# Attention and a two-layer network in one kernel: dummy matmuls, two attention blocks and two copies rearranged

## The chip, the cores and the metric

The kernel runs on one core of a Trainium2 chip. A core has TensorE (matmuls, written PE, with its weight loads as PEld), VectorE (DVE), ScalarE (ACT), GpSimd (POOL) and SyncE (SP), which run side by side and wait for each other by semaphores, and 16 DMA engines fed from queues on SP and POOL. Matmul results go to PSUM, which has eight banks of 2 KB for each of 128 partitions; everything else is in SBUF. The metric is the device time of one execution in microseconds; lower is better.

## The reference

What is computed, for 8 batches, 8 heads, 576 positions and 64 values per head:

```python
q_s = softmax(q, over the 64 values of a head)        # per position
k_s = softmax(k, over the 576 positions)              # per value
kv  = einsum('bhsd,bhse->bhde', k_s, v)               # 64 x 64 per head
x   = einsum('bhsd,bhde->bhse', q_s, kv)              # as 4608 rows of 512
h   = x @ w_in                                        # 512 x 2048
out = maximum(0.01 * h, h) @ w_out                    # 2048 x 512
```

Inputs and output are 4-byte floats. The softmaxes subtract their maximum first.

## The kernel before, in words

The 4608 rows are cut into nine blocks of 512 (NT; index t). The two matrices of the network stay in SBUF in bf16, and so does xT, the attention's output transposed. For a block, layer 1 makes 16 tiles of h (j = 0 to 15, each four matmuls, `layer1`), ScalarE applies the leaky function from PSUM to SBUF (`leaky`, tile gj), and layer 2 sums 16 matmuls for each of four groups of 128 rows (`layer2`, tsub 0 to 3) into a bank called pout; the result is copied by VectorE or ScalarE (`store`) and sent out from SP's queue.

A batch has 576 rows, so blocks and batches don't line up: block t has the last rows of batch t-1 and the first rows of batch t. The first stage takes all 576 rows of batch 0 (16 tiles of 256 columns in two halves, then 16 of 320); its last 64 rows are carried over to block 1 by `g_carry`, eight small POOL copies.

The attention of a batch: maxima and subtraction for k and q (VectorE and POOL), exponentials (ScalarE), v cast to bf16 with a column of ones (`v_cast`, tile vb), key-value product and sums of k on TensorE (`kv`, 36 small matmuls into two banks), their quotient (`kd_make`, tile kd, VectorE), q normalised and transposed by a DMA from SP's queue (`q_turn`, tile qX), and eight matmuls for the output (`attend_x`, two row ranges XR of 5 and 4 of the nine row groups, four head pairs each; tile po), each of which ScalarE or VectorE casts into xT. Batch 0 does its transposes on TensorE (`q_transpose`, `q_keep`) and its outputs in `attend`.

The order of all this is written out by hand. No scheduler moves anything: each engine runs its instructions in the order of the program. `at(t, u, ...)` hangs functions on a place in the loops, and `run(t, u)` calls them there. For t = 0, u is 0 to 15 in the 256-column stage, 16 to 31 in the 320-column stage and 32 to 47 in layer 2 (one u for each j, which is four matmuls). For later blocks u is 0 to 15 in layer 1 and 16 to 31 in layer 2 (four matmuls each). `plan2` hangs batch 2's steps on block 1, `plan` those of batches 3 to 7 on later blocks.

PSUM is in two pools: psB with six banks (name tag "bank2k": h tiles, po, key-value products, transposes) and psO with two (pout). In block 0 layer 2 sums four row groups at once: two in psO and two in psB (pout2), which leaves four psB banks for anything else until those are copied out.

Before the first real matmuls TensorE has dummies: `wake(n)` issues n bf16 matmuls of zeros, 128x512, into a bank that nobody reads, and `wake_on(x, n)` does the same behind a small matmul that reads x, so that it starts when x is there.

Of the kernel before, what the change touches and what calls it, by code (L numbers as in the profile page):

```python
# [8 lines left out]
FP32 = mybir.dt.float32  # L9
# [16 lines left out]
def kernel(  # L26
# [9 lines left out]
    nc = tc.nc  # L36
# [10 lines left out]
    P = 128  # L47
    NB = C // P
    NF = F // P
    TT = 512  # L50
# [4 lines left out]
    const_pool = ctx.enter_context(tc.tile_pool(name="const", bufs=1))  # L55
# [12 lines left out]
    psO_pool = ctx.enter_context(tc.tile_pool(name="psO", bufs=2, space=bass.MemoryType.PSUM))  # L68
# [19 lines left out]
    st = [{} for _ in range(B)]  # L88
# [15 lines left out]
    identf = const_pool.tile([P, P], FP32)  # L104
# [2 lines left out]
    nc.gpsimd.memset(block, 0.0)  # L107
    for p0 in range(0, P, D):
        nc.gpsimd.memset(block[p0 : p0 + D, p0 : p0 + D], 1.0)
    warm = const_pool.tile([P, 1], BF16)  # L110
    nc.scalar.activation(out=warm, in_=ident[:, 0:1], func=AF.Exp)
    gate = const_pool.tile([P, 1], FP32)
# [117 lines left out]
    def q_first(b, rs):  # L230

        n = rs.stop - rs.start
        nmax = small_pool.tile([P, HL, n], FP32, name="nmax")
        qsum = small_pool.tile([P, n, HL], FP32, name="qsum")
        for hs in (slice(0, 2), slice(2, 4)):
            nc.vector.tensor_reduce(
                out=nmax[:, hs], in_=st[b]["q"][:, hs, rs], axis=AX.X, op=ALU.max, negate=True
            )
            for h in range(hs.start, hs.stop):
                for r in range(n):  # L240
                    nc.scalar.activation(
                        out=st[b]["qe"][:, rs.start + r, h],
                        in_=st[b]["q"][:, h, rs.start + r],
                        func=AF.Exp,
                        bias=nmax[:, h, r : r + 1],
                        accum_out=qsum[:, r, h : h + 1],
                    )
        st[b]["qsum"] = qsum
        st[b]["nmax"] = nmax
# [41 lines left out]
    def kv(b):  # L291

        pkv = [psB_pool.tile([P, 2, 130], FP32, name="pkv", tag=BANK_TAG) for _ in range(2)]
        for gg in range(2):
            for r in range(R):
                for hh in range(2):
                    rows = slice(hh * L, (hh + 1) * L)
                    nc.tensor.matmul(  # L298
                        pkv[hh][:, gg, 0:129],
                        lhsT=st[b]["ke"][rows, r, 2 * gg : 2 * gg + 2].rearrange(  # L300
                            "p h d -> p (h d)"
                        ),
                        rhs=vb2[b % 2][rows, r, gg, 0:129],
                        start=(r == 0),
                        stop=(r == R - 1),
                    )
        st[b]["pkv"] = pkv

    def kd_make(b):
        for hh in range(2):  # L310
            pkv = st[b]["pkv"][hh]
            krec = small_pool.tile([P, 2, 1], FP32, name="krec")
            nc.vector.reciprocal(out=krec, in_=pkv[:, :, 128:129])
            for hp in range(2):
                p0 = hp * D
                nc.vector.tensor_tensor(
                    out=kd2[b % 2][p0 : p0 + D, 2 * hh : 2 * hh + 2, p0 : p0 + D],
                    in0=pkv[p0 : p0 + D, :, p0 : p0 + D],
                    in1=krec[p0 : p0 + D].to_broadcast([D, 2, D]),
                    op=ALU.mult,  # L320
                )

    wake_ps = psO_pool.tile([P, TT], FP32, name="pout")

    def wake(n):
        for i in range(n):
            nc.tensor.matmul(  # L327
                wake_ps, lhsT=zero[:, 0:P], rhs=zero, start=(i == 0), stop=(i == n - 1)
            )

    def wake_on(x, n):

        nc.tensor.matmul(wake_ps[:, 0:8], lhsT=identf, rhs=x, start=True, stop=True)
        wake(n)

    def k_max_pe(b, i):
        ps = psB_pool.tile([P, 2, L], FP32, name="kT", tag=BANK_TAG)
# [71 lines left out]
    def q_keep(eng, b, r0, n, ggs=(0, 1)):  # L409
        for gg in ggs:  # L410
            o, i = st[b]["qT", gg][:, :, r0 : r0 + n], st[b]["ps", r0][:, gg::2]
            if eng is nc.scalar:
                eng.copy(out=o, in_=i)
            else:
                eng.tensor_copy(out=o, in_=i)

    def attend(b, gs, c0, n, eng, pool=psB_pool, tag=BANK_TAG):

        ps = pool.tile([P, len(gs), n], FP32, name="po", tag=tag)
        for i, g in enumerate(gs):  # L420
            nc.tensor.matmul(
                ps[:, i],
                lhsT=kd2[b % 2][:, g],
                rhs=st[b]["qT", g % 2][:, g // 2].rearrange("c r l -> c (r l)")[:, c0 : c0 + n],
                start=True,
                stop=True,
            )
        x0 = XB[gs[0]]
        o = xT[:, x0 : x0 + len(gs), b * S + c0 : b * S + c0 + n]
        if eng is nc.scalar:  # L430
            eng.copy(out=o, in_=ps)
        else:
            eng.tensor_copy(out=o, in_=ps)
# [10 lines left out]
    def attend_x(b, g, rs, eng):  # L444
        hh, gg = divmod(g, 2)
        n = (rs.stop - rs.start) * L
        ps = psB_pool.tile([P, n], FP32, name="po", tag=BANK_TAG)
        qX = st[b]["qX"].rearrange("c (r g) (h l) -> c g h r l", g=2, h=2)
        nc.tensor.matmul(  # L449
            ps.rearrange("p (r l) -> p r l", l=L), lhsT=kd2[b % 2][:, g], rhs=qX[:, gg, hh, rs]  # L450
        )
        c0 = b * S + rs.start * L
        o = xT[:, XB[g], c0 : c0 + n]
        if eng is nc.scalar:
            eng.copy(out=o, in_=ps)  # L455
        else:
            eng.tensor_copy(out=o, in_=ps)
# [11 lines left out]
    def leaky(o, ph):  # L469
        nc.scalar.activation(out=o, in_=ph, func=AF.Prelu, alpha=LEAKY_SLOPE)  # L470
# [22 lines left out]
    def at(t, u, *fns):  # L493
        while t > 0 and u >= 32:
            t, u = t + 1, u - 32
        hooks.setdefault((t, u), []).extend(fns)
# [14 lines left out]
    XR = (slice(0, 5), slice(5, R))  # L511
# [3 lines left out]


    HA, HB = slice(0, 1), slice(1, 2)
    wake(13)
    nc.gpsimd.tensor_copy(out=gate[:, 0:1], in_=st[0]["k"][:, HL - 1, R - 1, D - 1 : D])
    load_w_in(0, 8)  # L520
    k_begin(0)
    q_begin(0)
    q_first(0, RA)
    wake_on(st[0]["nmax"].rearrange("p h r -> p (h r)")[:, 8:16], 3)
    k_tree(0, H0)
    k_max_pe(0, 0)
    wake(1)
# [10 lines left out]
    v_cast(nc.gpsimd, 0, 1)  # L538
    k_all_dve(0, 1)
    k_all_pe(0, 1)  # L540
    wake(5)
    k_sub_ps(0, 0, HB)
    k_exp(0, slice(1, 2))
    v_cast(nc.scalar, 0, 0)
# [36 lines left out]
        load_w_out(slice(j0, j1))  # L581


    at(0, 11, lambda: attend(0, [0, 2], 256, 256, nc.scalar))
    at(0, 11, lambda: attend(0, [1, 3], 256, 256, nc.vector))
    at(0, 11, lambda: attend(0, [0, 2, 1, 3], 512, 64, nc.scalar, psO_pool, "pout"))
    at(0, 15, lambda: k_begin(1), lambda: q_begin(1), lambda: k_tree(1, H0), lambda: k_tree(1, H1))
    at(0, 15, lambda: q_max(1, XR[0]), lambda: q_sub(nc.gpsimd, 1, XR[0]), lambda: k_allmax(1))
    at(0, 15, lambda: k_sub(nc.vector, 1, H0), lambda: k_sub(nc.vector, 1, H1))
# [5 lines left out]
    at(0, 39, lambda: kv(1), lambda: q_sum(1, XR[1]), lambda: q_norm(1, XR[1]), lambda: kd_make(1))  # L595
    at(0, 43, lambda: q_turn(1, XR[1]), lambda: load_all(2))
    for i in range(8):
        eng = nc.vector if i in (5, 7) else nc.scalar
        at(0, 47, lambda i=i, eng=eng: attend_x(1, i % 4, XR[i // 4], eng))


    for b in range(3, B):
# [20 lines left out]
    def plan2():  # L623
        b = 2
        at(1, 0, lambda: k_begin(b), lambda: q_begin(b), lambda: k_tree(b, ALLH))
        at(1, 3, lambda: k_allmax(b))
        at(1, 6, lambda: k_sub(nc.vector, b, H0), lambda: k_sub(nc.vector, b, H1))
        at(1, 12, lambda: k_exp(b, ALLH))
        for rs in XR:
            at(1, 9, lambda rs=rs: q_max(b, rs), lambda rs=rs: q_sub(nc.gpsimd, b, rs))  # L630
        at(1, 13, lambda: v_cast(nc.gpsimd, b, 0), lambda: v_cast(nc.gpsimd, b, 1))
        for i, rs in enumerate(XR):
            at(1, (15, 16)[i], lambda rs=rs: q_exp(b, rs), lambda rs=rs: q_sum(b, rs), lambda rs=rs: q_norm(b, rs))
            at(1, (16, 17)[i], lambda rs=rs: q_turn(b, rs))
        at(1, 21, lambda: kv(b))
        at(1, 22, lambda: kd_make(b))
        for i in range(8):
            at(1, 28 + i // 2, lambda i=i: attend_x(b, i % 4, XR[i // 4], nc.scalar))

# [13 lines left out]
            g_next.append(g_tile())  # L653
            nc.gpsimd.tensor_copy(out=g_next[jj][:, :, 0:L], in_=g_sb[jj][:, :, TT : TT + L])

    at(0, 46, g_carry)
    begun = []

    def begin(j):
# [12 lines left out]
    for j in range(0, NF, 2):  # L672
        if j == 8:
            q_transpose(0, 4, 2)
            for jj in range(8, NF, 2):
                begin(jj)
            q_keep(nc.vector, 0, 4, 2)
            q_transpose(0, 6, 3)
            q_keep(nc.vector, 0, 6, 3)
        ph = begun.pop(0)  # L680
        for i in range(2):
            layer1(j + i, ph[:, i], 0, 256, slice(2, 4), i == 0, i == 1)
            if i == 1:
                leaky(g_sb[j // 2][:, :, 0:256], ph)
            run(0, j + i)
# [5 lines left out]
    pout = [psO_pool.tile([P, O], FP32, name="pout") for _ in range(2)]  # L691
# [66 lines left out]
```

## Time and profile before

| what | value |
|---|---|
| median of three runs | 291.18 us (291.14 to 291.42) |
| profiled execution | 291.04 us |
| its span, first to last instruction | 289.2 us |
| granted TensorE clock, mean | 1.000 |
| TensorE busy | 279.7 us (97%) |
| ScalarE, VectorE, POOL busy | 148.2, 148.5, 85.6 us |
| HBM read, written | 36.70 MB, 9.44 MB |

The profile is of one execution. Times are microseconds from the first instruction. A line of a timeline has the start, the busy time, the engine, the line of the kernel, the operation, output and inputs, sizes, the count of instructions merged, and in brackets the idle time of the engine before it with what ended it. A record of a matmul goes from its start until its result has left the array, so neighbouring records overlap; the step from start to start is what a matmul takes in a stream (0.2155 us for 512 columns, 0.109 for 256). In a merged line the shape is that of the first instruction.

What waited for what on TensorE, added up over the run: the first dummy for POOL's zeros 1.3 us; the transpose of k's maxima for VectorE 0.9; batch 0's key-value product for ScalarE's cast of v 0.8; the broadcast of the maxima 0.7; layer 1 for w_in's load 0.7; batch 2's key-value product for POOL's cast of v 0.4; the dummies behind nmax 0.4; layer 1 for xT 0.2.

### The profile page before, as it was taken

The numbers are of one execution on the slowest core, as the hardware profiler recorded it, in microseconds if no ns is written. First come the engines' busy times: TensorE is split into PE (matmuls) and PEld (weight loads), VectorE is DVE, ScalarE is ACT, GpSimd is POOL, SyncE is SP. The second block draws the span as 40 slices with busy tenths as digits, with TensorE's granted clock in tenths as the row PEclk, the third lists the DMA queues.
The fourth block names the chain that finished last, engine by engine and source line by source line (L and its number), as shares of the span: only waits on it lengthen the run. The fifth ranks groups of instructions, "written<-read, shape, count | busy, mean of one in ns | idle before, by whom it ended". The sixth has DMA issues, their size and how long they took to land.

```text
span 289.2 us, 4274 instructions
## 1 busy us (share of the span) xinstructions
PE 279.7 (97%) x1646; PEld 138.5 (48%) x1646; DVE 148.5 (51%) x246; ACT 148.2 (51%) x273; POOL 85.6 (30%) x70
## 2 busy tenths in 40 slices
PE   7689999999999999999999999999999999999995
PEld 2277654454444544454454544444454444444443
DVE  3997883896880994388175637554631200110011
ACT  4976870785269307922774358433953066016400
POOL 4735460017059009505900590039100000000000
PEclk9999999999999999999999999999999999999999
DMA  7999996987749174953397239913141310131033
GB/s 257 314 208 378 258 189 186 399 293 296 148 108 399 62 154 118 398 133 76 78 381 187 50 82 348 239 36 73 39 82 36 75 36 1 36 82 29 0 72 75
DMA packets 38932, 46.35 MB, mean 160 GB/s; under 512 B 18304, under 2 KB 21632, under 8 KB 38912
## 3 DMA queue, kind: packets, MB, share of 16 engines
q1 hardware_dynamic: 35456, 41.75, 48.5%
q0 software_dynamic: 3296, 4.20, 8.3%
q8 instruction: 13, 0.21, 0.3%
q10 hardware_dynamic: 160, 0.13, 0.1%
q14 instruction: 7, 0.06, 0.1%
HBM read 36.70 MB, written 9.44 MB: 160 GB/s over the span
## 4 chain that ended last, share of the span: by engine, by line
PE 74%; POOL 1%; ACT 0%; DVE 0%; issue 0%
PE pout L482 37%; PE ph L461 34%; PE pkv L298 2%; PE po L449 2%; POOL vb L216 1%; ACT xT L455 0%; DVE out_sb L476 0%
## 5 line engine op out<-in xcount | busy, mean ns | idle before, releaser
L482 PE MATMUL pout<-w_out_sb,gj 128*128 128x512 bf16 (+2 forms) x592 | 130.0, 373 | 0.0
L461 PE MATMUL ph<-xT,w_in_sb 128*128 128x512 bf16 (+3 forms) x640 | 127.5, 358 | 1.2 <-DMA w_in_sb<-in_moe_w_in_dram 0.7
L470 ACT ACTIVATE gj<-ph 128x512 bf16<-128x512 f32 (+2 forms) x152 | 83.6, 581 | 57.8 <-PE ph L461 55.8
L461 PEld LDWEIGHTS <-w_in_sb 128*128 128x128 bf16 x640 | 62.1, 98 | 63.5 <-issue 2.4
L482 PEld LDWEIGHTS <-gj 128*128 128x128 bf16 x592 | 57.0, 98 | 62.5
L476 DVE COPY out_sb<-pout 128x512 f32<-128x512 f32 (+1 forms) x34 | 22.7, 675 | 85.4 <-PE pout L482 82.5
L196 POOL TENSOR_TENSOR k_raw<-k_raw,kall 128x2304 f32<-128x2304 f32 x5 | 25.3, 5066 | 76.8 <-DVE kall L188 50.4
L455 ACT CAST xT<-po 128x320 bf16<-128x320 f32 (+1 forms) x54 | 18.8, 405 | 48.4 <-PE po L449 48.4
L259 POOL TENSOR_TENSOR q_raw<-q_raw,qmax 128x2304 f32<-128x2304 f32 (+3 forms) x10 | 29.7, 2974 | 22.4 <-DVE qmax L228 22.4
L276 DVE TENSOR_REDUCE qsum<-qe 128x36 f32<-128x2304 bf16 (+4 forms) x11 | 19.8, 1798 | 32.2 <-ACT qe L267 32.2
L283 DVE TENSOR_TENSOR qe<-qe,qrec 128x2304 bf16<-128x2304 bf16 (+4 forms) x12 | 21.9, 1826 | 0.4
L204 ACT ACTIVATE ke<-k_raw 128x2304 bf16<-128x2304 f32 (+2 forms) x11 | 17.5, 1595 | 8.7 <-POOL k_raw L196 8.5
L228 DVE TENSOR_REDUCE qmax<-q_raw 128x36 f32<-128x2304 f32 (+4 forms) x11 | 19.6, 1788 | 0.0
L267 ACT ACTIVATE qe<-q_raw 128x2304 bf16<-128x2304 f32 (+4 forms) x11 | 16.8, 1526 | 1.5 <-POOL q_raw L259 1.3
L216 POOL CAST vb<-v_raw 128x1152 bf16<-128x1152 f32 x13 | 14.6, 1147 | 0.0
L449 PE MATMUL po<-qX,kd 128*128 128x320 bf16 (+1 forms) x56 | 11.6, 286 | 0.3
L163 DVE TENSOR_TENSOR t<-k_raw 128x1024 f32<-128x1024 f32 (+1 forms) x10 | 10.1, 1011 | 0.5 <-DMA k_raw<-in_k_dram 0.2
L327 PE MATMUL pout<-zero 128*128 128x512 bf16 x28 | 8.9, 443 | 1.3 <-POOL zero L101 1.3
L163 DVE TENSOR_TENSOR t<-t 128x256 f32<-128x256 f32 (+2 forms) x20 | 9.6, 478 | 0.7
L476 ACT COPY out_sb<-pout 128x512 f32<-128x512 f32 (+1 forms) x3 | 1.6, 543 | 15.6 <-PE pout L482 15.6
L298 PE MATMUL pkv<-vb,ke 64*128 64x129 bf16 x252 | 8.5, 216 | 0.4 <-POOL vb L216 0.4
L298 PEld LDWEIGHTS <-ke 64*128 64x128 bf16 x252 | 7.2, 93 | 3.5 <-ACT gj L470 1.7
(61 smaller groups left out, 100.3 us busy)
## 6 DMA issues: line engine op xcount, KB each, us to landing
out_dram<-out_sb SPq DMA_DIRECT2D x70, 128.0 KB, 2.4
q_raw<-in_q_dram SPq DMA_DIRECT2D x7, 1152.0 KB, 8.2
v_raw<-in_v_dram SPq DMA_DIRECT2D x7, 1152.0 KB, 11.5
k_raw<-in_k_dram SPq DMA_DIRECT2D x6, 1152.0 KB, 5.8
k_raw<-in_k_dram SPq DMA_DIRECT2D x4, 576.0 KB, 5.6
w_in_sb<-in_moe_w_in_dram POOLq DMA_DIRECT2D x8, 256.0 KB, 7.1
v_raw<-in_v_dram SPq DMA_DIRECT2D x2, 576.0 KB, 7.4
w_out_sb<-in_moe_w_out_dram POOLq DMA_DIRECT2D x4, 256.0 KB, 9.4
```

The costliest lines, as they stand in the source:

```text
L163: nc.vector.tensor_tensor(out=o, in0=i0, in1=i1, op=ALU.max)
L196: eng.tensor_tensor(out=ks, in0=ks, in1=st[b]["kall"][:, hs].unsqueeze(2).to_broadcast([P, n, R, D]), op=ALU.subtract,)
L228: nc.vector.tensor_reduce(out=m, in_=st[b]["q"][:, :, rs], axis=AX.X, op=ALU.max)
L259: eng.tensor_tensor(out=qs, in0=qs, in1=st[b]["qmax", rs.start].unsqueeze(3).to_broadcast([P, HL, n, D]), op=ALU.subtract,)
L276: nc.vector.reduce_sum(out=qsum, in_=st[b]["qe"][:, rs], axis=AX.X)
L283: nc.vector.tensor_tensor(out=qes, in0=qes, in1=st[b]["qrec", rs.start].unsqueeze(3).to_broadcast([P, n, HL, D]), op=ALU.mult,)
L298: nc.tensor.matmul(pkv[hh][:, gg, 0:129], lhsT=st[b]["ke"][rows, r, 2 * gg : 2 * gg + 2].rearrange("p h d -> p (h d)"), rhs=vb2[b % 2][row ...
L455: eng.copy(out=o, in_=ps)
L461: nc.tensor.matmul(ph, lhsT=w_in_sb[:, cb, j * P : (j + 1) * P], rhs=xT[:, XB[cb], c0 : c0 + n], start=(i == 0 and first), stop=(i == NB - ...
L470: nc.scalar.activation(out=o, in_=ph, func=AF.Prelu, alpha=LEAKY_SLOPE)
L476: copy(out=out_sb, in_=pout)
L482: nc.tensor.matmul(pout, lhsT=g_sb[j // 2][:, j % 2, tsub * P : (tsub + 1) * P], rhs=w_out_sb[:, j, os], start=(j == 0), stop=(j == NF - 1),)
```

## The change

Five edits:

- The dummies. `wake(13)` becomes `wake(6)` and one matmul of 4-byte zeros (`wake32`); `wake_on` becomes a single 4-byte matmul that reads x through a broadcast to 512 columns; `wake(5)` becomes one `wake32`. POOL fills the 4-byte zeros (zerof) once at the start.
- Batch 0's late rows: ScalarE copies the first half of each transposed q (head pairs 0 and 2), VectorE the second; before, VectorE copied both. The attention of rows 256 to 575 of batch 0 is hung on u = 9 in place of 11, ahead of three more h tiles.
- Batch 1's attention: four matmuls after j = 13 of layer 2 (u = 45) and four after j = 14 (u = 46); before, all eight after j = 15 (u = 47). ScalarE and VectorE take turns with the casts (before, six on ScalarE and two on VectorE), and head pairs go in the order 0, 2, 1, 3.
- `g_carry` is hung on u = 47 in place of 46.
- Batch 2's `kv` and `kd_make` are hung on u = 23 and 24 of block 1 in place of 21 and 22.

```diff
+    zerof = const_pool.tile([P, TT], FP32)
+    nc.gpsimd.memset(zerof, 0.0)
...
-    def wake_on(x, n):
-
-        nc.tensor.matmul(wake_ps[:, 0:8], lhsT=identf, rhs=x, start=True, stop=True)
-        wake(n)
+    def wake32():
+        nc.tensor.matmul(wake_ps, lhsT=zerof[:, 0:P], rhs=zerof, start=True, stop=True)
+
+    def wake_on(x):
+
+        nc.tensor.matmul(
+            wake_ps.rearrange("p (a b) -> p a b", b=64),
+            lhsT=zerof[:, 0:P],
+            rhs=x.unsqueeze(2).to_broadcast([P, 8, 64]),
+            start=True,
+            stop=True,
+        )
...
-    wake(13)
+    wake(6)
+    wake32()
...
-    wake_on(st[0]["nmax"].rearrange("p h r -> p (h r)")[:, 8:16], 3)
+    wake_on(st[0]["nmax"].rearrange("p h r -> p (h r)")[:, 8:16])
...
-    wake(5)
+    wake32()
...
-    at(0, 11, lambda: attend(0, [0, 2], 256, 256, nc.scalar))
-    at(0, 11, lambda: attend(0, [1, 3], 256, 256, nc.vector))
-    at(0, 11, lambda: attend(0, [0, 2, 1, 3], 512, 64, nc.scalar, psO_pool, "pout"))
+    at(0, 9, lambda: attend(0, [0, 2], 256, 256, nc.scalar))
+    at(0, 9, lambda: attend(0, [1, 3], 256, 256, nc.vector))
+    at(0, 9, lambda: attend(0, [0, 2, 1, 3], 512, 64, nc.scalar, psO_pool, "pout"))
...
-        eng = nc.vector if i in (5, 7) else nc.scalar
-        at(0, 47, lambda i=i, eng=eng: attend_x(1, i % 4, XR[i // 4], eng))
+        eng = (nc.scalar, nc.vector)[i % 2]
+        at(0, (45, 46)[i // 4], lambda i=i, eng=eng: attend_x(1, (0, 2, 1, 3)[i % 4], XR[i // 4], eng))
...
-        at(1, 21, lambda: kv(b))
-        at(1, 22, lambda: kd_make(b))
+        at(1, 23, lambda: kv(b))
+        at(1, 24, lambda: kd_make(b))
...
-    at(0, 46, g_carry)
+    at(0, 47, g_carry)
...
-            q_keep(nc.vector, 0, 4, 2)
+            q_keep(nc.scalar, 0, 4, 2, (0,))
+            q_keep(nc.vector, 0, 4, 2, (1,))
             q_transpose(0, 6, 3)
-            q_keep(nc.vector, 0, 6, 3)
+            q_keep(nc.scalar, 0, 6, 3, (0,))
+            q_keep(nc.vector, 0, 6, 3, (1,))
```

## The prediction

> **What bounds the kernel now.** I read the page's busy table and its chain first, then TensorE's own timeline for gaps, then the timelines of the engines that end each gap.
>
> ```profile
> PE 279.7 (97%) x1646; PEld 138.5 (48%) x1646; DVE 148.5 (51%) x246; ACT 148.2 (51%) x273; POOL 85.6 (30%) x70
> PE 74%; POOL 1%; ACT 0%; DVE 0%; issue 0%
> ```
>
> The chain that ended last is TensorE alone from 70.6 us to the end, apart from 0.4 us at 81 us and the last copy. So a change gains only where TensorE waits, and what it gains once stays gained if no later wait takes it. TensorE's timeline shows the places:
>
> ```profile
> 25.11 9.96 PE L461 MATMUL ph<-xT,w_in_sb 128*128 128x256 bf16 x72
> ...
> 26.21 0.70 PE L461 MATMUL ph<-xT,w_in_sb 128*128 128x320 bf16 x4
> ...
> 41.91 1.20 PE L298 MATMUL pkv<-vb,ke 64*128 64x129 bf16 x36
> 43.03 7.08 PE L482 MATMUL pout<-w_out_sb,gj 128*128 128x512 bf16 x32
> 49.95 2.07 PE L449 MATMUL po<-qX,kd 128*128 128x320 bf16 x8
> 52.03 8.19 PE L461 MATMUL ph<-xT,w_in_sb 128*128 128x448 bf16 x42
> 64.22 5.34 PE L482 MATMUL pout<-w_out_sb,gj 128*128 128x512 bf16 x24
> 69.55 0.69 PE L298 MATMUL pkv<-vb,ke 64*128 64x129 bf16 x18
> 70.64 0.69 PE L298 MATMUL pkv<-vb,ke 64*128 64x129 bf16 x18 [0.41 <-POOL vb L216]
> 99.41 1.20 PE L298 MATMUL pkv<-vb,ke 64*128 64x129 bf16 x36
> 100.54 7.08 PE L482 MATMUL pout<-w_out_sb,gj 128*128 128x512 bf16 x32
> ```
>
> To be seen: the 320-column stage starts only once a cast on ScalarE (25.76 to 26.16) is done; batch 1's eight attention matmuls hold TensorE from 49.95 to 52.03 though the chain charges such pairs 0.27 us (320 columns) and 0.22 us (256); batch 2's key-value product takes 71.26-69.55 = 1.71 us where batch 3's takes 100.54-99.41 = 1.13 us. Who ends these waits:
>
> ```profile
> 25.76 0.41 ACT L431 CAST xT<-po 128x256 bf16<-128x256 f32 x1
> ...
> 50.29 1.97 ACT L455 CAST xT<-po 128x320 bf16<-128x320 f32 x6 [8.44 <-PE po L449]
> 51.40 0.42 DVE L457 CAST xT<-po 128x256 bf16<-128x256 f32 x1 [5.21 <-PE po L449]
> 52.06 0.42 DVE L457 CAST xT<-po 128x256 bf16<-128x256 f32 x1 [0.23 <-PE po L449]
> 52.40 2.47 DVE L476 COPY out_sb<-pout 128x512 f32<-128x512 f32 x4
> 68.35 2.24 POOL L216 CAST vb<-v_raw 128x1152 bf16<-128x1152 f32 x2
> ```
>
> Six of eight evacuations stand in a row on ScalarE, 0.32 us apart, and the last four matmuls wait for banks: two of psB's six hold layer-2 sums, so four are left for eight results. At 69.55 the wait is for POOL's two casts of v.
>
> **The change part by part.**
>
> *Dummies, before 13.3 us.* Thirteen become six and one 4-byte; 1+3 become one 4-byte on nmax; five become one 4-byte. No row has a 4-byte 128x512 matmul. Below: two passes at the bf16 rate of 0.216 us (a 4-byte matmul shows as two records), 0.43 us. Above: the pair of 4-byte 128-column matmuls at 8.99 us holds TensorE 0.37 us; four times that, 1.5 us. I take 0.9, between them, since half of the short row is load and latency. At either end nothing waits: the first starts at 3.9 us and ends by 5.6, while nmax comes at 6.1; the second runs 6.12 to at most 7.6, while kmax comes at 8.06; the third 11.2 to at most 12.7, while ScalarE's cast of v ends at 13.2 (kv starts at 13.27 and waited 0.80 us). Cost 0, if the clock stays up (rival 1).
>
> *POOL's memset of zerof*: 0.5 us (rows of 128x512: 0.52, 0.56), at most 1.1 at twice the bytes. It delays four memsets on POOL's queue, the last ending at 4.0 us; POOL then idles to 7.75. The new dummy can wait 0.1 us for it. Cost 0.
>
> *q's late rows and hook 11 to 9.* Now VectorE copies both halves of rows 6 to 8 in 0.62 us from 23.60; after, ScalarE does one at the same time: its 512-column copy took 0.58 us, its 256-column cast 0.41, so about 0.49, ready at 24.1. TensorE does j=8's second half (four matmuls, 0.44 us) from 23.69 to 24.13 and goes to the attention with at most 0.03 us of wait. On ScalarE only j=8's leaky stands behind that waiting copy, and its matmuls end at 24.29 anyway; the leakies from j=10 on now stand behind two casts, and their banks are not needed before 27.6. What is gained: the 320-column layer 1 waited for the last xT cast (ScalarE, ends 26.16) and began at 26.21, though the eight matmuls of j=12 and 14, 0.109 apart from 25.11, had ended at 25.98. After: attention 24.15 to 24.71 (its 0.55 us), then j=10 to 14, twelve matmuls of 0.109, to 26.02. The casts start behind j=8's leaky, at 24.82 in place of 25.29, and are done by 25.7. Start 26.02 in place of 26.21: gain 0.19. The ends: 0 (a late copy) and 0.22 (no wait). The next inputs, w_out's loads, land 7.7 to 13.8 us after their issues from 25.36: the first by 33.1 (used at 34.7), the second by about 35.5 (36.4). Covered.
>
> *Batch 1 in two groups.* Needed work: 2x0.27+2x0.22 = 0.98 us; taken 2.08: 1.10 waits. At 52.03 the first 448-column matmuls wait another 0.09 for casts. After: group one at 49.76-8x0.2155 = 48.03. Its inputs: kd done at 46.2; the first transpose, issued at 40.77, and the second, at 44.72, each about 3.4 us to landing, so 44.4 and 48.1. Four banks, four results, no wait. One j (0.86 us), group two at 49.43. Its banks: ScalarE frees one at 48.8 and 49.1, VectorE one at about 49.0 and 49.45 (0.49 us for 320, between its 0.42 for 256 and 0.69 for 512); the fourth is wanted at 49.76. Then j=15 until 50.73 hides the second casts, done about 50.6. Gain 1.10+0.09 = 1.19; bounds 0.5 (VectorE's casts twice as long) and 1.19. g_carry moves by one hook; its POOL copies keep their queue order and wait for the same layer-2 steps: 0. No DMA moves on SP's queue or POOL's, and behind the casts ScalarE and VectorE hold only work that needs j=15 or layer 1.
>
> *Batch 2's key-value product, two hooks later.* Its stall is 1.71-1.13 = 0.58. TensorE arrives now at 69.4, after at 69.4-0.19-1.19+8x0.2155 = 69.74. The casts hang on VectorE: its four stores ran from 52.40, behind the last batch-1 cast; after, from about 50.6, so the maxima of batch 2 start at 53.0 for 54.91, and the casts end at 68.7 for 70.59. Even with no shift the second half waits only 0.28. Gain 0.58, lower bound 0.3. What is late next: kd_make and the attention of batch 2. TensorE reaches that at 77.36-1.38-0.58 less 0.2 for rounding of starts, about 75.2; kd was done at 76.14, and shifts with VectorE by 1.8 to about 74.4; qX's first transpose, issued 72.08, about 3.4 us on, shifts to 73.7. It fits by 0.8 us, only because the chain shifts.
>
> From 77.4 on every engine follows TensorE, so the 0.4 us at 81 stays and so do the gains.
>
> **Sum:** 0.19+1.19+0.58 = 1.96 us. Profiled execution: 291.04 us, span 289.2 and 1.84 around it; 291.04-1.96 = 289.08. The median of the runs, 291.18, stands 0.14 above, so 289.2.
>
> [...] The clock rose before TensorE had been busy 3.0 us:
>
> ```profile
> 3.85 0.15 PEld L327 LDWEIGHTS <-zero 128*128 128x128 bf16 x1 [0.28 <-issue]
> 4.28 0.99 PEld L327 LDWEIGHTS <-zero 128*128 128x128 bf16 x5 [0.28 <-issue]
> ```
>
> Dummies came 0.43 us apart until 4.28 and 0.2 apart after, from a start at 1.32. [...]
>
> **Rivals.**
>
> 1. *The clock does not rise, or falls again* (slower). Cover runs 1.32 to 5.0 in place of 5.6, then a gap to 6.1; if 4-byte passes count for less, 2.6 us of bf16 fall short of the 3.0 seen. Against: 4.3 lies inside the new cover, and 7.7 to 11.2 was half idle without a fall. Price: dummies at half rate delay kT by 0 to 1.8 us; TensorE's work from 13.3 to 16.6, busy 2.6 us, up to doubles; 3 us of layer 1 at half rate lose 1.5, of which the waits for w_in at 21 and 23.5 (0.66+0.27) swallow 0.9. Between 0.5 and 4.5; I take 2.9: 292.1. It decides above 2.0.
> 2. *The evacuations stay late*: VectorE's casts, or group two's banks, hold TensorE as before. Gain 0.5 in place of 1.19: 289.9.
> 3. *Batch 2's chain does not shift*: it is held by its loads of k and q (issued 46.06 and 46.68), POOL's casts stay at 70.6 and kd at 76.1. Then kv waits 0.28 and the attention 1.0: 290.4. Against: VectorE began on k straight after its stores.
> 4. *Absorbed*: the gains come back at a fixed transfer, as w_out's loads or batch 3's: 291.1. Against: from 81.4 on the chain has no wait at all.
>
> **How the numbers follow.** Forecast 0.74, rival 1 0.07, rival 2 0.07, rival 3 0.08, rival 4 0.04. Forecast alone: 288.8 to 289.7 (all upper ends; the lower ends of two terms). The range goes up to 290.3, taking in rival 2; below, 288.7. 0.2% is 0.58 us, about what measurement can tell from no change. Faster: forecast, rivals 2 and 3, 0.89. Same: rival 4, 0.04. Slower: rival 1, 0.07.
>
> **What would show it.** TensorE's timeline: attention in two groups of four near 48.0 and 49.4, each about half a microsecond, layer 1 of the next block at about 50.7; one unbroken pkv of 36 near 69.7; the 320-column stage at 26.0; dummies at 0.43 us until about 4.3. Wrong would be: 0.43 us spacing, or 0.2 us for 256 columns, later than 8 us; a wait on xT or vb where none is forecast; or po of batch 2 waiting for kd near 75.

## The result, and the profile after

The changed kernel takes **289.49 us** (median; 289.12 to 291.79) against 291.13 (290.74 to 291.54) for the kernel before beside it: a ratio of **0.9949 [0.9938, 0.9960]**, a gain of 1.64 us where the forecast had 1.96 from its sum. The profiled execution is 289.72 us, with a span of 287.9. The page's busy table, clock row and chain by engine, of the changed kernel:

```profile
PE 278.1 (97%) x1609; PEld 138.6 (48%) x1635; DVE 149.1 (52%) x246; ACT 148.1 (51%) x273; POOL 86.1 (30%) x71
...
PEclk9799999999999999999999999999999999999999
...
PE 89%; DMA 5%; POOL 2%; DVE 1%; issue 1%; ACT 0%; SPq 0%; ACTq 0%; POOLq 0%
```

One thing differs from before: the second slice of the clock row is a 7, since the clock fell once after it had risen. TensorE is at 97%, as before. (The chain shows more here because it reaches back to the first loads; the chain of the kernel before began at 68.41 with POOL's casts of v, and its shares leave out what came earlier.) TensorE's own timeline of the changed kernel (start, length, instruction, tile, count, and in brackets the wait ahead of it):

```profile
1.32 2.74 PE L329 MATMUL pout<-zero 128*128 128x512 bf16 x6 [1.32 <-POOL zero L101]
3.85 1.86 PE L334 MATMUL pout<-zerof 128*128 128x512 f32 x2
6.07 1.12 PE L338 MATMUL pout<-nmax,zerof 128*128 128x512 f32 x2 [0.36 <-DVE nmax L238]
8.10 0.33 PE L348 MATMUL kT<-identf,kmax 128*128 128x128 f32 x1 [0.91 <-DVE kmax L165]
...
17.26 1.03 PE L471 MATMUL ph<-xT,w_in_sb 128*128 128x256 bf16 x8 [0.24 <-ACT xT L441]
...
24.44 0.60 PE L471 MATMUL ph<-xT,w_in_sb 128*128 128x256 bf16 x4 [0.93 <-DMA w_in_sb<-in_moe_w_in_dram]
...
48.75 0.71 PE L459 MATMUL po<-qX,kd 128*128 128x320 bf16 x4
49.30 1.03 PE L492 MATMUL pout<-w_out_sb,gj 128*128 128x512 bf16 x4
50.16 0.60 PE L459 MATMUL po<-qX,kd 128*128 128x256 bf16 x4
50.60 1.03 PE L492 MATMUL pout<-w_out_sb,gj 128*128 128x512 bf16 x4
51.46 12.27 PE L471 MATMUL ph<-xT,w_in_sb 128*128 128x448 bf16 x64
...
70.57 1.19 PE L300 MATMUL pkv<-vb,ke 64*128 64x129 bf16 x36
71.70 4.49 PE L492 MATMUL pout<-w_out_sb,gj 128*128 128x512 bf16 x19
76.02 0.43 PE L459 MATMUL po<-qX,kd 128*128 128x320 bf16 x2
```

The rows of the kernel before with which this is compared, beside those shown in the prediction:

```profile
16.57 1.03 PE L461 MATMUL ph<-xT,w_in_sb 128*128 128x256 bf16 x8 [0.24 <-ACT xT L431]
...
23.69 1.03 PE L461 MATMUL ph<-xT,w_in_sb 128*128 128x256 bf16 x8
...
77.32 0.44 PE L449 MATMUL po<-qX,kd 128*128 128x320 bf16 x2
```

From the bottom up: batch 2's key-value product is one unbroken run of 36, and its 1.71 us are now 71.70 − 70.57 = 1.13. Batch 1's attention is two groups of four that hold TensorE for 0.55 and 0.44 us, instead of one block of 2.08. Both moves do what was forecast. But block 0 starts late: its first layer 1 at 17.26 (before 16.57), and j=8's second half, at 24.44, ended a wait of 0.93 for w_in (before 23.69). So the main part starts with a loss of 0.75 us; at block 1's layer 1 the kernel is ahead by 52.03 − 51.46 = 0.57 and at batch 2's attention by 77.32 − 76.02 = 1.30, which is what the spans differ by (289.2 − 287.9).

Where the start was lost is in the view by stretches (from:to, length, then busy time and count of PE, PEld, DVE, ACT and POOL, then the granted clock, DMA share, GB/s), of the changed kernel:

```profile
1.30:5.50 4.20, 4.18 (x8) 1.39 (x8) 0.76 (x2) 0.96 (x3) 2.88 (x12) 1.00 0.81 265
5.60:8.90 3.30, 1.79 (x5) 0.46 (x4) 2.94 (x8) 3.30 (x21) 1.12 (x3) 1.00 1.05 399
9.00:12.30 3.30, 3.27 (x13) 1.50 (x14) 2.72 (x7) 2.83 (x14) 2.87 (x5) 0.50 1.09 349
```

and two of the same stretches of the kernel before:

```profile
5.60:8.90 3.30, 1.73 (x8) 0.59 (x7) 2.93 (x8) 3.30 (x21) 1.16 (x3) 1.00 1.06 398
9.00:12.30 3.30, 2.97 (x17) 1.06 (x17) 3.23 (x7) 3.21 (x15) 2.83 (x5) 1.00 1.09 343
```

The clock column (the first of the last three) is the reading: 0.50 from 9.00 to 12.30 where it was 1.00. By the clock's own records it rose at 5.54, fell at 8.95 and rose again at 12.36. (The column's 1.00 in the first stretch is not to be trusted, since dummies still came 0.43 us apart there.) With half the clock the dummies at 9.65 and 10.05 are 0.40 us apart, the second broadcast of k's maxima came at 11.28 in place of 10.84 and ended at 11.98 in place of 11.28. VectorE's last subtraction from k, which reads it, ended at 13.43 in place of 12.74, and POOL's gate for the second half of w_in followed at 13.57 in place of 12.87. The chain's pieces (start, length, what) show what that made late:

```profile
14.03 1.29 POOL w_in_sb L136 x3
15.77 8.53 DMA w_in_sb<-in_moe_w_in_dram
```

POOL began to issue w_in's second half at 14.03 (13.33 before), and its last piece landed at 24.31 (23.55 before). Not all of the 0.75 is the fall: in another profile of the changed kernel, whose clock held (the run `after_again` below), POOL began at 13.39, the last piece landed at 23.74 and j=8's second half started at 23.88, which is still 0.19 behind the kernel before.

The clock's fall is not in every execution. Of 20 executions of the changed kernel seven have a mean clock of 0.987 to 0.994 and a median of 290.11 us; the other thirteen have 0.998 or more and a median of 289.34. The profile above is one of the seven. So the median of all holds about 0.15 us of it, and with a clock that holds the gain is 291.13 − 289.34 = 1.79. One stretch of 3.41 us at half clock in a span of 288 us makes a mean clock of 0.994, two make 0.988. By that, four of the seven had one such stretch and three (0.987, 0.988 and 0.988) two; no profile of those three is kept.

### The profile page after: what moved, and what is told of

Its sections match the earlier page's. It is cut to its first block, busy times and chain, and to the rows that moved or that the text cites. A ratio compares the mean times of both kernels' runs of the same rounds, so it can differ in the third digit from the quotient of the medians.

```text
span 287.9 us, 4226 instructions
## 1 busy us (share of the span) xinstructions
PE 278.1 (97%) x1609; PEld 138.6 (48%) x1635; DVE 149.1 (52%) x246; ACT 148.1 (51%) x273; POOL 86.1 (30%) x71
## 4 chain that ended last, share of the span: by engine, by line
PE 89%; DMA 5%; POOL 2%; DVE 1%; issue 1%; ACT 0%; SPq 0%; ACTq 0%; POOLq 0%
PE pout L492 43%; PE ph L471 41%; DMA w_in_sb<-in_moe_w_in_dram 3%; PE pkv L300 3%; PE po L459 2%; DMA k_raw<-in_k_dram 2%; POOL w_in_sb L136 1%; DVE t L165 1%; DVE k_raw L374 0%; POOL vb L218 0%; ACT gj L480 0%; PE po L431 0%; SPq L79 0%; ACT xT L465 0%; DVE kmax L165 0%
## 5 line engine op out<-in xcount | busy, mean ns | idle before, releaser
L465 ACT CAST xT<-po 128x320 bf16<-128x320 f32 (+1 forms) x52 | 18.2, 402 | 48.6 <-PE po L459 48.6
L459 PEld LDWEIGHTS <-kd 128*128 128x128 bf16 x56 | 5.5, 98 | 6.2
L318 DVE TENSOR_TENSOR kd<-pkv,krec 64x128 bf16<-64x128 f32 x28 | 8.1, 289 | 0.7
```

The lines of the kernel that those rows point to most:

```text
L459: nc.tensor.matmul(ps.rearrange("p (r l) -> p r l", l=L), lhsT=kd2[b % 2][:, g], rhs=qX[:, gg, hh, rs])
```

## The experiments

Three questions were open: what each part of the change is worth, whether the gains add, and what the clock's fall comes from. Each expectation tells its theories apart by numbers. All times are medians beside runs of the kernel before on the same chip (291.15, 291.02 or 291.09, by the chip).

### The change with the dummies of before

```diff
-    wake(6)
-    wake32()
+    wake(13)
-    wake_on(st[0]["nmax"].rearrange("p h r -> p (h r)")[:, 8:16])
+    wake_on(st[0]["nmax"].rearrange("p h r -> p (h r)")[:, 8:16], 3)
-    wake32()
+    wake(5)
```

(with `zerof` and its memset gone and `wake_on` as it was).

> The changed kernel with the dummies of the kernel before. Theory A (the three moves give 1.96 us as summed, and the new dummies take some of it back, because the clock falls in some executions, as from 8.95 to 12.36 us in the changed kernel's profile): about 289.2 us where the changed kernel had 289.5, no stretch at clock 0.5, and all executions close together. Theory B (the dummies cost nothing; the 0.3 us that are missing were mis-sized in the moves): 289.5 us, and as much scatter as the changed kernel.

Measured: 289.27 (288.48 to 289.78), 0.9938 [0.9926, 0.9950], a gain of 1.88, with a mean clock of 0.998 or more in all six executions. Its interval overlaps that of the changed kernel, so the medians alone don't part the two; the clocks do. The time lies 0.07 from that of the thirteen executions whose clock held (289.34), so no cost of the new dummies is to be seen when it does. Theory A's other sign did not come: the executions are 1.3 us apart, not close together, though the clock held in all of them.

### The new dummies alone

```diff
+    zerof = const_pool.tile([P, TT], FP32)
+    nc.gpsimd.memset(zerof, 0.0)
...
-    wake(13)
+    wake(6)
+    wake32()
...
-    wake_on(st[0]["nmax"].rearrange("p h r -> p (h r)")[:, 8:16], 3)
+    wake_on(st[0]["nmax"].rearrange("p h r -> p (h r)")[:, 8:16])
...
-    wake(5)
+    wake32()
```

on the kernel before, with the new `wake32` and `wake_on`, and nothing else.

> The kernel before with the new dummies alone. Theory A: slower than before by 0.1 to 0.4 us in the median, with a third of the executions at a mean clock of 0.994 or less and those some 0.8 us longer than the rest. Theory B: 291.1 us, the same as before, whatever the clock.

Measured: 291.24 (291.14 to 291.94), 1.0009 [1.0001, 1.0018]: a loss of 0.09 us, at the edge of what can be told. One of eleven executions shows the fall (mean clock 0.992, and the slowest, 291.94), where theory A said a third. TensorE's timeline in its profile, where the clock held:

```profile
6.15 1.13 PE L338 MATMUL pout<-nmax,zerof 128*128 128x512 f32 x2 [0.38 <-DVE nmax L238]
...
16.68 1.03 PE L471 MATMUL ph<-xT,w_in_sb 128*128 128x256 bf16 x8 [0.24 <-ACT xT L441]
```

The whole 4-byte matmul on nmax takes 1.13 us from its start to its last result, and layer 1 starts at 16.68 against 16.57. That is not the dummies' doing: k's loads landed 0.13 later in this execution (the first at 6.31, 6.18 before), and the transpose of k's maxima started at 8.19 in place of 8.06. The dummies are off the path, as forecast; the fall is what they can cost.

### Batch 1 in two groups alone

```diff
-        eng = nc.vector if i in (5, 7) else nc.scalar
-        at(0, 47, lambda i=i, eng=eng: attend_x(1, i % 4, XR[i // 4], eng))
+        eng = (nc.scalar, nc.vector)[i % 2]
+        at(0, (45, 46)[i // 4], lambda i=i, eng=eng: attend_x(1, (0, 2, 1, 3)[i % 4], XR[i // 4], eng))
-    at(0, 46, g_carry)
+    at(0, 47, g_carry)
```

> The kernel before with batch 1's attention in two groups (and the carry copies one hook later) alone. By the sum of the prediction 1.19 us less than before, 289.9 us, and attention matmuls in two groups of about half a microsecond. Rival 2 (the evacuations stay late): 0.5 us less, 290.6, with waits of TensorE left inside the second group or at layer 1 behind it.

Measured: 289.37 (289.08 to 289.99), 0.9945 [0.9933, 0.9957], a gain of 1.78 (by its interval 1.25 to 1.95) where its own term was 1.19. This one edit brings nearly the whole of the change. TensorE's timeline of this kernel:

```profile
48.27 0.71 PE L449 MATMUL po<-qX,kd 128*128 128x320 bf16 x4
...
49.68 0.60 PE L449 MATMUL po<-qX,kd 128*128 128x256 bf16 x4
...
50.98 12.27 PE L461 MATMUL ph<-xT,w_in_sb 128*128 128x448 bf16 x64
...
68.36 1.34 PE L298 MATMUL pkv<-vb,ke 64*128 64x129 bf16 x36
...
75.68 0.43 PE L449 MATMUL po<-qX,kd 128*128 128x320 bf16 x2
```

and, from the timelines of VectorE and POOL of the same kernel, the casts of batch 1's results, the stores behind them, and the casts of v for batch 2:

```profile
48.75 0.89 DVE L457 CAST xT<-po 128x320 bf16<-128x320 f32 x2 [2.51 <-PE po L449]
50.10 0.76 DVE L457 CAST xT<-po 128x256 bf16<-128x256 f32 x2 [0.47 <-PE po L449]
50.77 2.47 DVE L476 COPY out_sb<-pout 128x512 f32<-128x512 f32 x4
...
66.72 2.24 POOL L216 CAST vb<-v_raw 128x1152 bf16<-128x1152 f32 x2
```

At its own place the edit brings what was forecast: layer 1 of block 1 starts 52.03 − 50.98 = 1.05 earlier. Then it brings more. From there to batch 2's attention it is 24.70 us (50.98 to 75.68) where it was 25.29 (52.03 to 77.32): another 0.59. Of this 0.14 comes ahead of the key-value product (50.98 to 68.36 against 52.03 to 69.55, the wait for casts in layer 1, forecast as 0.09), and 0.45 is most of the product's stall (68.36 to 75.68 against 69.55 to 77.32); its 36 matmuls are now one run without a wait for vb. The reason stands in the second fence. VectorE's stores start at 50.77, which is 1.63 us before the 52.40 of the kernel before, and POOL's casts of v start at 66.72, 1.63 before 68.35. TensorE itself came only 1.19 earlier to the key-value product (69.55 to 68.36). The chain that makes vb gained 0.44 on TensorE, as much as the stall lost.

### Batch 2's key-value product later, alone

```diff
-        at(1, 21, lambda: kv(b))
-        at(1, 22, lambda: kd_make(b))
+        at(1, 23, lambda: kv(b))
+        at(1, 24, lambda: kd_make(b))
```

> The kernel before with batch 2's key-value product two hooks later alone. By the sum 0.58 us less, 290.55 us: TensorE reaches it at 71.1, after the casts of v that end at 70.6, and the product runs in one piece of 36. Rival 3 says that without the shift of VectorE's chain the attention of batch 2 waits for its inputs in its place: TensorE gets there at 76.8, kd is done at 76.1, so by rows no wait; if it waits all the same, 291.1.

Measured: 290.40 (290.09 to 290.71), 0.9975 [0.9966, 0.9984], a gain of 0.75, by its interval 0.47 to 0.99; the term was 0.58. TensorE's timeline of this kernel:

```profile
71.22 1.20 PE L298 MATMUL pkv<-vb,ke 64*128 64x129 bf16 x36
72.36 4.49 PE L482 MATMUL pout<-w_out_sb,gj 128*128 128x512 bf16 x19
76.68 0.43 PE L449 MATMUL po<-qX,kd 128*128 128x320 bf16 x2
```

72.36 − 71.22 = 1.14 in place of 1.71, and the attention comes 77.32 − 76.68 = 0.64 earlier: the term is right where the edit stands alone.

The two edits alone sum to 1.78 + 0.75 = 2.53, more than both with everything else (1.88 with the old dummies, by its interval 1.46 to 2.15). So they don't add: both remove the same stall.

### All of it but the key-value move

The change with the old dummies, and

```diff
-        at(1, 23, lambda: kv(b))
-        at(1, 24, lambda: kd_make(b))
+        at(1, 21, lambda: kv(b))
+        at(1, 22, lambda: kd_make(b))
```

> The changed kernel with the old dummies and with batch 2's key-value product back where it was. Theory C (the moves overlap: batch 1's grouping alone gave 1.78 us and left no wait at batch 2's product, because VectorE's chain for batch 2 came forward by more than TensorE): 289.3 us, the same as with the later product, and no wait for vb. The prediction's sum, in which the product's 0.58 us is a gain of its own: 289.85 us, and a wait near 68.4 us.

Measured: 289.35 (289.14 to 289.61), 0.9945 [0.9932, 0.9957]. With the move it was 0.9938 [0.9926, 0.9950]: no difference that can be told. TensorE's timeline of this kernel, and what is left of the stall:

```profile
68.45 1.33 PE L298 MATMUL pkv<-vb,ke 64*128 64x129 bf16 x36
```

1.33 us for the run of 36 against 1.19 with the move (70.57, above): 0.14 us is what the move is still worth once batch 1 is in two groups. The theory that the moves overlap (theory C) holds.

### q's late rows alone

```diff
-    at(0, 11, lambda: attend(0, [0, 2], 256, 256, nc.scalar))
+    at(0, 9, lambda: attend(0, [0, 2], 256, 256, nc.scalar))
...
-            q_keep(nc.vector, 0, 4, 2)
+            q_keep(nc.scalar, 0, 4, 2, (0,))
+            q_keep(nc.vector, 0, 4, 2, (1,))
             q_transpose(0, 6, 3)
-            q_keep(nc.vector, 0, 6, 3)
+            q_keep(nc.scalar, 0, 6, 3, (0,))
+            q_keep(nc.vector, 0, 6, 3, (1,))
```

(all three `attend` lines of hook 11 go to 9.)

> The kernel before with the split copy of q's late rows and the attention of batch 0 two hooks earlier, alone. By the prediction's term 0.19 us less than before: 290.95 us, with the 320-column stage starting some 0.2 us earlier after the last weights of w_in have landed. Theory C adds: VectorE's chain does not come forward by more than that, so nothing more is gained. If the term is nought, 291.15.

Measured: 291.05 (290.86 to 291.37), 1.0002 [0.9994, 1.0011]: nothing that can be told, where the term was 0.19. The timelines of ScalarE and VectorE of this kernel:

```profile
23.62 0.48 ACT L413 COPY qT<-psum_qt 128x384 bf16<-128x384 bf16 x1 [1.91 <-PE psum_qt L397]
...
24.13 0.36 DVE L415 COPY qT<-psum_qt 128x384 bf16<-128x384 bf16 x1 [1.63 <-ACT qT L413]
```

The two copies don't run at the same time. VectorE's bracket names ScalarE's copy: the two halves lie in one tile (psum_qt), which is one bank of PSUM, and the second reader waited for the first (24.13 behind 24.10). (Whether the wait goes by tile or by bank, no run here tells.) Both are done at 24.49 in place of the 24.1 of the forecast, later than VectorE alone had them (23.60 + 0.62 = 24.22). The second pair of attention matmuls then waits, from 24.37 to 24.55, and the 320-column stage starts 2.50 us after j=8's second half, where it was 26.21 − 23.69 = 2.52.

That is not what happened in the changed kernel's own profile, with the same copies:

```profile
23.55 0.48 ACT L423 COPY qT<-psum_qt 128x384 bf16<-128x384 bf16 x1 [1.19 <-PE psum_qt L407]
...
24.06 0.36 DVE L425 COPY qT<-psum_qt 128x384 bf16<-128x384 bf16 x1 [0.91 <-ACT qT L423]
```

They too run one behind the other, but there TensorE stood still for w_in's last piece until 24.44 (the 0.93 above), and both copies were done at 24.42, ahead of the attention at 24.88. The 320-column stage began at 26.74, 2.30 after j=8's second half: a gain of 0.23 at the place. So the late copy costs the gain only where TensorE does not wait for w_in just then. Of the eight profiles with the split copies and hook 9, five have that wait, of 0.9 to 1.3 us, and 2.30 (the run with the new dummies alone has the same wait, and 2.52); the other three, in which TensorE waited for an earlier piece, have 2.50, 2.56 and 2.64.

### Hook 9 alone

```diff
-    at(0, 11, lambda: attend(0, [0, 2], 256, 256, nc.scalar))
-    at(0, 11, lambda: attend(0, [1, 3], 256, 256, nc.vector))
-    at(0, 11, lambda: attend(0, [0, 2, 1, 3], 512, 64, nc.scalar, psO_pool, "pout"))
+    at(0, 9, lambda: attend(0, [0, 2], 256, 256, nc.scalar))
+    at(0, 9, lambda: attend(0, [1, 3], 256, 256, nc.vector))
+    at(0, 9, lambda: attend(0, [0, 2, 1, 3], 512, 64, nc.scalar, psO_pool, "pout"))
```

on the kernel before; VectorE makes both copies.

> The kernel before with the attention of batch 0 two hooks earlier alone, VectorE copying both halves of q's late rows as before. Theory D (in the run with the split copy the gain was lost because VectorE's copy waited for ScalarE's, though both only read the bank): the second attention matmuls no longer wait, the 320-column stage begins 0.15 to 0.2 us earlier after w_in has landed, 290.85 us where before has 291.02. If the gain was lost elsewhere: the second group still starts 0.18 us late and the time stays at 291.0.

Measured: 291.03 (290.70 to 291.41), 0.9997 [0.9988, 1.0006]: not told apart from no change. In its profile q's transposes came at 23.35 in place of 23.07, so VectorE's copies were late as well (23.88), and the 320-column stage began 2.44 after j=8: the gain at the place was 0.08 in that execution, and the run can't say more. Of theory D's two numbers, 290.85 and 291.0, the total is the second, the one against it; the interval takes in both.

### The gap between the dummies filled

```diff
     wake_on(st[0]["nmax"].rearrange("p h r -> p (h r)")[:, 8:16])
+    wake(4)
```

on the changed kernel. TensorE has no work there from 7.2 to 8.1 us.

> The changed kernel with four bf16 dummies more behind the one that waits for nmax, which cover the gap from 7.0 to 8.1 us. Theory A (the clock falls because a stretch of 3.4 us had too little TensorE work in it): no execution at a mean clock under 0.997, and a median of 289.3. If something else than the work in that stretch lets the clock fall (4-byte matmuls as such, say), a third of the executions still stand at 0.994 or less.

Measured: 289.34 (288.95 to 290.88), 0.9949 [0.9932, 0.9966], no fall in six executions. The slowest one, which is the profiled one, had k's load late by 0.9 us and so all that follows; its clock held.

### The changed kernel and the filled one once more, side by side

The same two kernels, on one chip.

> The changed kernel again, beside the filled one on the same chip. Theory A: a third of the executions at a mean clock of 0.994 or less, and those 0.5 to 1 us longer than the rest; the rest at 289.35.

> The changed kernel with four bf16 dummies more behind the one that waits for nmax, again. Theory A: no execution under 0.997, median 289.3. If 4-byte matmuls as such let the clock fall, as many low ones as in the changed kernel beside it.

Measured: the changed kernel 289.15 (288.97 to 289.57), 0.9936 [0.9924, 0.9949]; the filled one 289.16 (289.03 to 289.65), 0.9936 [0.9924, 0.9949]. Neither showed a fall, in five executions each, where theory A said a third for the changed kernel. So these two don't settle it: the changed kernel without a fall is as fast as the filled one, and whether the filled one never falls stays open by count (none of 11, where with the new dummies without the filling the clock fell in 8 of 36 in all: 7 of the first 20, and 1 of the 16 after them). With a clock that held, the changed kernel's gain here is 1.94.

### Batch 2's attention in three, three and two

Old dummies, and

```diff
-            at(1, 28 + i // 2, lambda i=i: attend_x(b, i % 4, XR[i // 4], nc.scalar))
+            at(1, 28 + i * 3 // 8, lambda i=i: attend_x(b, (0, 2, 1, 3)[i % 4], XR[i // 4], nc.scalar))
```

so that one j of layer 2 lies between the last casts and block 2's layer 1.

> The changed kernel with the old dummies, and batch 2's eight attention matmuls as three, three and two after the first, second and third step of the last row group, in the order 0, 2, 1, 3, in place of two after each step. The wait of 0.4 us at the start of block 2's layer 1 (81.0 to 81.4 in the profile before) should go: 0.4 us less than the old dummies' 289.27, 288.9. If the earlier matmuls wait for kd or for the transposes in its place, 289.3 or more.

Measured: 288.86 (288.74 to 289.21), 0.9930 [0.9918, 0.9942]. TensorE's timeline of this kernel:

```profile
77.09 0.52 PE L449 MATMUL po<-qX,kd 128*128 128x320 bf16 x3
...
78.31 0.38 PE L449 MATMUL po<-qX,kd 128*128 128x256 bf16 x2
78.52 1.03 PE L482 MATMUL pout<-w_out_sb,gj 128*128 128x512 bf16 x4
79.39 4.91 PE L461 MATMUL ph<-xT,w_in_sb 128*128 128x512 bf16 x21
```

and of the one it is built on, the change with the old dummies:

```profile
78.77 0.38 PE L449 MATMUL po<-qX,kd 128*128 128x256 bf16 x2
78.99 5.21 PE L461 MATMUL ph<-xT,w_in_sb 128*128 128x512 bf16 x21
```

The first 21 matmuls of block 2's layer 1 take 4.91 us in place of 5.21: most of the 0.4 us for the last casts, which the prediction left standing at 81 us, is gone. Against the kernel before on its own chip the gain is 2.16 where it was 1.88: 0.28 more, which agrees.

### The best of the parts together

The last kernel, with

```diff
-            q_keep(nc.scalar, 0, 4, 2, (0,))
-            q_keep(nc.vector, 0, 4, 2, (1,))
+            q_keep(nc.vector, 0, 4, 2)
             q_transpose(0, 6, 3)
-            q_keep(nc.scalar, 0, 6, 3, (0,))
-            q_keep(nc.vector, 0, 6, 3, (1,))
+            q_keep(nc.vector, 0, 6, 3)
```

and hook 9 kept.

> The kernel before with batch 1 in two groups, batch 0's attention two hooks earlier, batch 2's attention matmuls in three, three and two; old dummies, old copies of q's late rows, batch 2's product where it was before or after (after). Theories C and D: 0.15 us less than the 288.86 with the split copy, 288.7. If the split copy was no loss: 288.9.

Measured: **288.75** (288.65 to 288.82), 0.9918 [0.9905, 0.9932]: 2.34 us under the kernel before, and the fastest of all. VectorE's timeline of this kernel:

```profile
23.68 0.62 DVE L415 COPY qT<-psum_qt 128x384 bf16<-128x384 bf16 x2 [0.95 <-PE psum_qt L397]
```

Both copies are done in one go from 23.68 to 24.30, 0.19 earlier than the end of the split pair in the run with q's late rows alone; the eight attention matmuls run without a wait from 24.14, and the 320-column stage starts 2.31 after j=8, which is the forecast's 0.19 and a little more (0.21), here with no wait for w_in just ahead of j=8. By the times, its gain over the kernel that it is built on (288.86, on another chip) is inside both intervals: seen at its place, not measured in the total.

## Why the prediction was right or wrong

- **The total and its sign** were right: 289.49 against 289.2, inside 288.7 to 290.3. Not all that was said for the terms was: the clock, q's late rows and the place of the 0.58 were wrong.
- **The dummies, cost 0.** Right for their lengths. The 4-byte matmul, taken as 0.9 us between 0.43 and 1.5, has two records 0.53 us apart and is 1.12 us from the first start to the last end; it holds TensorE until 7.2, and kmax came at 8.1. Wrong for the clock: rival 1, given 0.07, came true in 7 of 20 executions of the first comparison. Its size was off too: taken as 2.9 us, it cost 290.11 − 289.34 = 0.8 by the medians, because the fall lay ahead of the main part and only w_in's loads carried it on (one execution did lose 2.4).
- **What failed in arguing against rival 1** was "7.7 to 11.2 was half idle without a fall". That stretch held more work than the new one: TensorE was busy 2.42 of its 3.50 us, against 1.85 of the 3.41 before the fall. I worked this out afterwards from the matmul records of fourteen profiles (this case's 12 experiments, before and after), as the time in which columns stream: 0.216 us for 512 columns in bf16, twice that for each record of a 4-byte one (at half clock such records start 0.85 us apart, bf16 ones 0.43). Cut into pieces of 3.41 us, the time from the rise to the fall in the changed kernel's profile, counted from each profile's rise, the piece in which the changed kernel's clock fell (5.54 to 8.95) held about 1.2 us; the next lowest of all pieces up to 23 us held 1.3 to 1.5, by whether matmuls that run side by side (the pairs that broadcast k's maxima, which start 0.007 us apart) are counted once or twice (7.37 to 10.78 in the run of three, three and two), and its clock did not fall. By the profile's busy time the order is the same: 1.85 and 2.06 us of 3.41. So a limit between 1.2 and 1.3 (1.5 by the second way of counting) would part all of them: an estimate from these profiles, with one fall among them. Counted from no rise it doesn't part them: from 5.60 to 8.90 the kernel before was busy 1.73 us, less than the 1.79 of the changed kernel, and kept its clock; its pieces, from 4.32 and from 7.73, were busy 2.46 and 2.37. With the dummies of before none of the 113 executions whose clock is on record fell. How often the new set falls short would, by this estimate, depend on the moment of the rise. Laid beside other rises, the records of the changed kernel give a piece of under 1.35 us from about 5.3 to 5.7 and of under 1.5 from about 4.4 to 5.8, which is an estimate of 0.1 to 0.4 for the share of executions; 8 of 36 were seen. With the filled kernel's four dummies, 0.86 us more, the same estimate gives 2.1 or more at every rise. All this is argued from the records, not tried by itself, and it does not say why three of the executions lost two stretches.
- **The rise taken as fixed.** The prediction took the one rise seen at 4.3 as fixed. Over fourteen profiles with the same start it came anywhere from 3.95 to 7.01 us, so it should have been a spread. In the one profile of a fall the clock fell 3.41 us after its rise (8.95 − 5.54) and stayed down as long (12.36 − 8.95); TensorE was busy 1.85 of the 3.41 us ahead of it.
- **q's late rows, 0.19.** The size came true in the changed kernel's own profile (0.23 at the place), but not for the reason given: the step that failed is "ScalarE does one at the same time". In all eight profiles with the split copies VectorE's comes behind ScalarE's (24.13 behind 24.10, 24.06 behind 24.03). The gain was there only where TensorE stood 0.9 us or more for w_in's last piece, on which the term did not count; without that wait it was 0.03, −0.04 and −0.12. That part is luck. The range had 0 as its lower end, "a late copy", but no reason for it. Here the two reads of one bank stood one behind the other. The trace shows the program's wait; no run here shows what happens without it. With VectorE keeping both copies the gain of the earlier hook is there at its place without a wait for w_in (0.21, in the kernel of the best parts).
- **Batch 1 in two groups, 1.19.** Right at its place: layer 1 of block 1 came 1.05 earlier in the run of this edit alone, though j=8 was 0.05 later there, and the waits for casts inside that layer went as well: no wait for a bank, no wait for casts. The two groups at 48.27 and 49.68 stand 0.24 and 0.25 behind the forecast 48.03 and 49.43, 0.19 of which is the term for q's rows that this kernel has not. Rival 2 (late evacuations) did not come.
- **Batch 2's key-value product, 0.58.** Right alone (0.64 at its place), wrong as a separate gain of that edit. The prediction had all it needed: it said that VectorE's stores come forward to about 50.6 and POOL's casts with them to 68.7 (seen alone: 50.77, and 66.72 + 2.24 = 68.96). It then counted the stall's end under the key-value move, though casts that come forward by 1.6 against a TensorE that comes forward by 1.2 cure most of it unaided. The sum survived since the 0.58 was counted once. In the changed kernel the move makes 0.14 of it.
- **Rivals 3 and 4** did not come: the chain of batch 2 did shift, and the gains were not given back at a later transfer. kd was done at 74.4 before its use at 75.42 in the run with the old dummies, a fit by 1.0 where 0.8 was forecast.

**The account.** The profiles let the gains be read at their places, as what each stretch of TensorE's timeline became shorter (a loss is negative). The stretches end at j=8's second half (23.69 before), at the 320-column stage (26.21), at layer 1 of block 1 (52.03) and at batch 2's attention (77.32):

| | start to j=8 | to 320 columns | to block 1 | to batch 2's attention |
|---|---|---|---|---|
| forecast | 0 | 0.19 | 1.10 | 0.09 + 0.58 |
| changed kernel, clock fell | −0.75 | 0.23 | 1.09 | 0.72 |
| changed kernel, clock held | −0.19 | 0.23 | 1.09 | 0.72 |
| old dummies | 0.12 | −0.04 | 1.09 | 0.72 |
| batch 1 alone | −0.05 | 0.00 | 1.10 | 0.59 |
| key-value product alone | 0.00 | 0.00 | 0.00 | 0.64 |

Behind j=8 the changed kernel gained 2.04, where the sum was 1.96; ahead of it, it lost time in w_in's arrival. So the median's 1.64 does not tell of a term that is missing: as far as the profiles show, the 0.3 us lie ahead of j=8, in part with the falls (0.15 of the median), in part with the moment at which w_in's last piece lands (23.44 to 23.91 us over twelve profiles, leaving out the fall's and the one with k's load late).

## What to carry to other kernels

- Before gains are added, ask of each stall whether another edit of the same change already removes it: a stall is a race between two chains, and an edit that brings forward the late chain by more than TensorE ends it without being aimed at it.
- Before a copy is split over two engines, see whether its halves lie in one tile of one bank: here they then ran one behind the other (24.13 behind 24.10), and the bracket of the second copy names the first. Halves in different banks were not tried.
- Read a gain at its place, from one fixed point of the timeline to the next, before it is looked for in the total: the total also holds when the loads happened to land.
- Before dummy work is thinned, lay what is left of it beside every moment at which the clock's rise was seen, and not the one of a single profile: here it came from 3.95 to 7.01 us, and the one fall in a profile came behind 3.41 us in which TensorE was busy 1.85. What it loses showed in 8 of 36 executions, so look at the mean clock of each.

## What the runs showed of the hardware that was not expected

- The clock fell for 3.41 us after a stretch in which TensorE was busy 1.85 of 3.41 us, and in the one profile of it, it rose again after those 3.41 us, in which TensorE was busy 3.33 at half rate. By their mean clocks (0.987 and 0.988) three other executions lost about twice as much.
- The first rise came between 3.95 and 7.01 us over fourteen profiles whose first dummy starts at 1.32 in each.
- A 4-byte 128x512 matmul is two records. They start 0.85 us apart at half clock and 0.53 apart at full clock, with zeros on the right side as with nmax, broadcast.
